# Memory attention and a bilinear feed-forward on one core: one block of ones for two buffers, and a new order of all units behind the first eighth

## The chip, the cores and the metric

The kernel runs on one core of a Trainium2 chip. The metric is the device time of one execution in microseconds (us), the median of several runs. TensorE is called PE, VectorE DVE, ScalarE ACT, GpSimd POOL and SyncE SP, as in the profile.

## The reference

Attention over 32 memory slots for 8 batches of 8 heads, 576 tokens of 64 numbers; its output is 4608 rows of 512, which go through a bilinear feed-forward with 1536 inner columns.

```python
a = np.exp(phi - max(phi)); a = a / sum(a)          # over the tokens
k_m = einsum('bhsm,bhsd->bhmd', a, k)               # 32 slots for each head
v_m = einsum('bhsm,bhsd->bhmd', a, v)
scores = q @ k_m^T / 8
attn = softmax(scores)                              # over the 32 slots
x = (attn @ v_m), heads side by side                # 4608 x 512
out = ((x @ w_a) * (x @ w_b)) @ w_out               # 512 -> 1536 -> 512
```

## The kernel before

The work runs batch by batch (b = 0 to 7). The attention's last product is never made alone: v_m is multiplied into w_a and w_b first ("folds", L516), so that one product of the softmax `A` with the folded weights `vab` gives the rows of `x @ w_a` and `x @ w_b`. The down projection with w_out takes blocks of 128 tokens in pairs, by seven products in the place of eight (L654); it needs sums of weights (L621) and of tokens (L638). For batches 5 to 7 most up projections are made by seven products too (L750), with sums of `vab` (L533) and of `A` (L541).

The ones: the sums over tokens of `a` come out of the same matmuls as k_m, since each buffer `kv_sb` holds three planes: k, v, and a constant (1/16). There are two such buffers, for even and odd b, and each has its constant plane; the first is written by VectorE (L236), the second by GpSimd (unit M, L792).

Nothing is ordered by a scheduler at run time: the string PLAN lists all units, and the loop at L785 records them in that order. Each engine then works through its own queue in that order, and waits by semaphore where it needs another's result. The names of units:

- `wa..`, `wb..`, `oN`, `pb`, `kb`, `vb`, `qb`: loads of w_a, w_b, w_out, phi, k, v, q, all issued by GpSimd's queue; at most eight of them are in flight, a ninth waits for the first to land.
- `2exp0`: exponentials of phi for b=2 (ACT); `2kv`: the sums with k, v and ones (PE, L323); `2km0`, `2km1`: their scaling (DVE); `2kvt`: transposes; `2qt0` to `2qt3`: transposes of q (DVE).
- `2sc`, `2e0`, `2den0`, `2nr0`: scores, exponentials, denominators and normalising; the last is a product on DVE for b below 2 and on POOL for b=2 and 3. From b=4 on `ed`, `sm`, `tn`, `ad` do it by transposes and row sums.
- `2v0a`, `2x0a0`: a fold into the first third of w_a, and one copy of it from PSUM.
- `a1.4.0`, `b1.4.0`: up projections with w_a and w_b (two matmuls each, L727) for batch 1, inner block 4, first half of the tokens; `a` is copied by ACT (L731), `b` multiplied by DVE into `ht` (L734).
- `P5.4.1`: one of the seven products; `H5.4` or `J5.4`: its closing product on POOL or DVE (L781).
- `V20`, `T30`: sums of w_out on DVE or POOL (quarter and half of it follow the letter); `5S01D`, `5S31P`: sums of `vab` on DVE or POOL; `5T0P`, `5T0D`: sums of `A` likewise.
- `g0.1`, `h0.1`: the sums of tokens for the pair of blocks 0, the second of four, on DVE or POOL.
- `d7`: the next seven matmuls of the down projection, 42 for each pair of blocks; after every sixth a result is taken by ACT or DVE.

```python
for x in PLAN.split():
    ...
    elif x[0] in "TV":
        sum_weights(int(x[1]), int(x[2]), nc.gpsimd if x[0] == "T" else nc.vector)
    elif x[0] in "hg":
        n, y = arg.split(".")
        sum_tokens(int(n), int(y), nc.gpsimd if x[0] == "h" else nc.vector)
    elif x[0] == "d":
        for _ in range(int(arg)):
            next(down)
```

Of the kernel before, what the change touches and what calls it, by code (L numbers as in the profile page):

```python
# [8 lines left out]
F32 = mybir.dt.float32  # L9
F16 = mybir.dt.float16  # L10
# [3 lines left out]
P = 128  # L14
# [9 lines left out]
1qh10 1qh00 o0 o3 1sh0 1eh00 0v1b 1v1b 1x0b1 1eh10 1x0a1 0x1b0 1den00 0x1b1 1x1b1 o4 1den10 o2 a0.6.1 b0.6.0 b0.6.1
b0.5.1 1nr10 1nr00 1x1b0 b0.4.0 a0.7.1 b0.7.1 a0.7.0 a0.5.0 b0.7.0 a1.5.0 b0.5.0 h0.3 b1.5.0 a1.3.0 1qh21 a0.4.1 o5
b1.3.0 1qh31 1qh01 a1.4.0 b0.4.1 a1.1.0 1qh11 a1.2.0 b1.4.0 a1.0.0 b1.1.0 1sh1 0v2a 1eh01 1eh11 0x2a1 b1.0.0 0x2a0
b1.2.0 1den01 a1.6.0 0v2b 0x2b0 0x2b1 b1.6.0 v2 a0.9.1 1v2b 1v2a 1x2b0 1x2b1 a0.11.1 1x2a1 1x2a0 b0.9.1 a0.10.1
a0.9.0 b0.11.1 b0.10.1 b0.9.0 V20 1den11 a1.10.0 b1.10.0 a0.11.0 b0.11.0 a0.8.0 a1.11.0 b0.8.0 b1.11.0 1nr11 d1
# [5 lines left out]
g2.3 2x2b1 3km0 2nr1 2x2b0 2x1a1 d7 3km1 d6 3qt2 2x1a0 2v0b 2v2a 2x0b1 3qt3 d3 3qt0 2x2a1 d3 a2.6.0 d1 b2.6.0 d1
3qt1 a2.4.0 2x2a0 b2.4.0 d1 h2.2 d1 a2.7.0 d2 a2.4.1 d1 2x0b0 b2.4.1 d4 a2.3.0 a2.1.1 3kvt 5exp1 v5 b2.7.0 p4 b2.3.0
a2.8.0 b2.1.1 k5 a2.1.0 d2 a2.2.0 d2 q4 d1 a2.5.0 h3.3 3sc 3e0 d2 b2.2.0 d1 3e1 d2 b2.8.0 5exp0 d1 b2.1.0 v4 d2
a2.10.0 d2 b2.10.0 a2.0.1 a2.11.0 b2.11.0 b2.5.0 3den0 a2.0.0 d1 b2.0.1 h3.0 d1 g3.1 a2.5.1 d1 a2.9.0 k4 b2.5.1 h3.2
b2.0.0 3nr0 a2.11.1 d1 a2.8.1 b2.9.0 d1 3den1 d2 a2.10.1 d2 b2.10.1 d1 3v0a 3nr1 3x0a1 5kv 3x0a0 3v0b 3x0b0 b2.8.1
# [35 lines left out]
a7.9.0 d1 P7.5.3 d2 P7.5.7 d1 J7.7 d1 g14.1 d1 P7.6.6 d1 P7.1.1 P7.6.5 P7.6.2 d1 7S20P d1 h14.2 P7.5.4 d3 P7.6.7
H7.5 d1 b7.11.0 P7.1.6 d1 h14.3 P7.1.5 P7.6.3 d1 P7.1.2 d2 P7.6.4 d1 P7.0.1 d1 P7.1.7 d1 H7.6 d1 b7.9.0 d1 P7.0.5 d1
P7.0.2 d1 P7.1.3 P7.0.6 d2 P7.1.4 P7.2.1 d2 P7.0.3 P7.3.1 d3 P7.0.7 P7.2.2 P7.2.6 P7.3.5 d3 P7.3.6 d2 J7.0 P7.2.5
P7.0.4 d1 H7.1 P7.2.7 d1 a7.10.1 P7.3.7 d5 P7.3.2 d2 P7.2.4 d3 P7.3.4 g15.0 d1 a7.8.1 d3 a7.9.1 g15.1 a7.11.1
b7.11.1 b7.9.1 d12 g15.2 g15.3 P7.2.3 b7.8.1 P7.3.3 d12 b7.10.1 d1 J7.3 H7.2 g16.0 d7 g16.1 g16.2 g16.3 g17.0 g17.1
d2 h17.2 d20 h17.3 d66
"""  # L80
# [3 lines left out]
def kernel(  # L84
# [196 lines left out]
    def units(b):  # L281
# [269 lines left out]
        def one(f, *a):  # L551
            return lambda: f(*a)
# [289 lines left out]
```

## Time and profile before

| what | value |
|---|---|
| median of 3 runs | 234.03 us (233.72 to 235.49) |
| profiled execution: span from first to last instruction | 232.1 us |
| PE busy | 214.1 us (92%) |
| DVE busy | 195.7 us (84%) |
| ACT busy | 169.4 us (73%) |
| POOL busy | 138.2 us (60%) |
| granted PE clock | 1.0 in all slices |

The profiled execution's own time is known by its span alone; the runs have 1.9 us more, which lies around it. A duration in a row is that of one instruction or of a merged run of them; PE's matmuls overlap, so that the distance between starts tells what one costs. Lines are those of the kernel before.

### The profile page before, as it was taken

The numbers are of one execution on the slowest core, as the hardware profiler recorded it, in microseconds if no ns is written. First come the engines' busy times: TensorE is split into PE (matmuls) and PEld (weight loads), VectorE is DVE, ScalarE is ACT, GpSimd is POOL, SyncE is SP. The second block draws the span as 40 slices with busy tenths as digits, with TensorE's granted clock in tenths as the row PEclk, the third lists the DMA queues.
The fourth block names the chain that finished last, engine by engine and source line by source line (L and its number), as shares of the span: only waits on it lengthen the run. The fifth ranks groups of instructions, "written<-read, shape, count | busy, mean of one in ns | idle before, by whom it ended". The sixth has DMA issues, their size and how long they took to land.

```text
span 232.1 us, 7493 instructions
## 1 busy us (share of the span) xinstructions
PE 214.1 (92%) x2906; PEld 163.6 (70%) x2906; DVE 195.7 (84%) x517; ACT 169.4 (73%) x450; POOL 138.2 (60%) x139
## 2 busy tenths in 40 slices
PE   1189879999999998999999999999999999999993
PEld 0143537588778777777777787887778877888882
DVE  3543899999987667898988999999999999999942
ACT  2206679987899997589978996977897769785330
POOL 7927233812549597893374099499475991881151
PEclk9999999999999999999999999999999999999999
DMA  6999999999998999999840902121303303032164
GB/s 229 238 199 256 205 205 205 205 259 258 208 284 138 264 207 243 253 241 254 210 93 4 190 1 65 28 64 32 93 3 90 78 16 92 18 77 55 42 158 111
DMA packets 26259, 34.09 MB, mean 147 GB/s; under 512 B 2000, under 2 KB 20304, under 8 KB 26224
## 3 DMA queue, kind: packets, MB, share of 16 engines
q0 software_dynamic: 19760, 23.14, 53.5%
q1 hardware_dynamic: 5952, 9.70, 16.2%
q10 hardware_dynamic: 512, 0.79, 1.0%
q8 instruction: 22, 0.36, 0.6%
q14 instruction: 13, 0.11, 0.1%
HBM read 42.47 MB, written 9.44 MB: 224 GB/s over the span
## 4 chain that ended last, share of the span: by engine, by line
PE 71%; DMA 17%; POOL 6%; ACT 3%; issue 2%; DVE 1%; POOLq 0%
PE py L654 18%; PE pb L727 11%; PE pa L727 11%; PE pv L654 9%; DMA wb_sb<-in_moe_w_b_dram 6%; DMA kv_sb<-in_k_dram 6%; PE py L750 5%; PE px L654 4%; PE pva L516 4%; DMA kv_sb<-in_v_dram 4%; PE pv L750 3%; POOL h_sums L638 2%; PE pkv L323 2%; PE px L750 1%; ACT vab L548 1%
## 5 line engine op out<-in xcount | busy, mean ns | idle before, releaser
L734 DVE TENSOR_TENSOR ht<-a_sb,pb 128x288 f16<-128x288 f16 (+2 forms) x144 | 60.5, 445 | 9.6 <-PE pb L727 5.3
L727 PEld LDWEIGHTS <-vab 128*128 128x128 f16 x576 | 55.3, 98 | 14.9 <-issue 2.4
L731 ACT CAST a_sb<-pa 128x288 f16<-128x288 f32 (+2 forms) x144 | 55.1, 417 | 13.6 <-PE pa L727 8.9
L727 PE MATMUL pb<-A,vab 128*128 128x288 f16 (+2 forms) x288 | 54.9, 286 | 0.1
L727 PE MATMUL pa<-A,vab 128*128 128x288 f16 (+2 forms) x288 | 54.3, 286 | 0.5 <-DVE A L478 0.4
L548 ACT CAST vab<-pva 128x512 f16<-128x512 f32 x82 | 45.4, 611 | 6.9 <-PE pva L516 6.8
L654 PEld LDWEIGHTS <-h_sums 128*128 128x128 f16 x432 | 41.4, 98 | 9.9 <-issue 2.4
L638 POOL TENSOR_TENSOR h_sums<-ht 128x768 f16<-128x768 f16 x19 | 31.2, 1645 | 21.4 <-DVE ht L734 21.3
L654 PE MATMUL py<-w_sums,h_sums 128*128 128x256 f16 x216 | 38.1, 273 | 0.0
L654 PEld LDWEIGHTS <-ht 128*128 128x128 f16 x324 | 31.2, 98 | 7.5 <-issue 2.2
L654 PE MATMUL pv<-wo_sb,h_sums 128*128 128x256 f16 x216 | 36.4, 273 | 0.0
L638 POOL TENSOR_TENSOR h_sums<-ht,h_sums 128x768 f16<-128x768 f16 x10 | 16.4, 1640 | 11.6 <-DVE h_sums L638 11.5
L755 ACT COPY z<-py 128x288 f32<-128x288 f32 x48 | 19.2, 415 | 2.3 <-PE py L750 1.8
L781 POOL TENSOR_TENSOR ht<-ah,bh 128x288 f16<-128x288 f16 x19 | 13.7, 737 | 10.1 <-DVE ah L759 7.1
L654 PE MATMUL px<-wo_sb,ht 128*128 128x256 f16 x108 | 18.9, 273 | 0.0
L654 PE MATMUL py<-wo_sb,ht 128*128 128x256 f16 x108 | 18.8, 273 | 0.0
L654 PE MATMUL py<-w_sums,ht 128*128 128x256 f16 x108 | 18.4, 273 | 0.0
L661 ACT ACTIVATE u<-py 128x256 f32<-128x256 f32 x36 | 14.4, 399 | 4.0 <-PE py L654 3.9
L425 ACT ACTIVATE E<-pscore 128x288 f16<-128x288 f32 x28 | 9.8, 431 | 9.5 <-PE pscore L412 9.4
L291 ACT ACTIVATE exp_sb<-phi_sb 128x576 f16<-128x576 f32 x16 | 10.9, 692 | 5.2 <-DMA phi_sb<-in_phi_dram 5.2
L300 DVE STREAM_TRANSPOSE qT<-q_sb 128x288 f32<-128x288 f32 x28 | 12.2, 456 | 2.6 <-DMA q_sb<-in_q_dram 2.6
L750 PE MATMUL py<-asum,vab 128*128 128x288 f16 x48 | 13.5, 286 | 0.0
(106 smaller groups left out, 383.0 us busy)
## 6 DMA issues: line engine op xcount, KB each, us to landing
out_dram<-o_sb SPq DMA_DIRECT2D x68, 128.0 KB, 2.4
phi_sb<-in_phi_dram POOLq DMA_DIRECT2D x8, 576.0 KB, 10.3
kv_sb<-in_v_dram POOLq DMA_DIRECT2D x8, 576.0 KB, 11.2
kv_sb<-in_k_dram POOLq DMA_DIRECT2D x7, 576.0 KB, 13.5
q_sb<-in_q_dram POOLq DMA_DIRECT2D x6, 576.0 KB, 11.9
wo_sb<-in_moe_w_out_dram POOLq DMA_DIRECT2D x6, 256.0 KB, 14.0
wa_sb<-in_moe_w_a_dram POOLq DMA_DIRECT2D x2, 512.0 KB, 14.2
wb_sb<-in_moe_w_b_dram POOLq DMA_DIRECT2D x2, 512.0 KB, 16.6
```

The costliest lines, as they stand in the source:

```text
L291: nc.scalar.activation(out=t["exp"][:, 2 * z:2 * z + 2, :, :], in_=phis[b][:, 2 * z:2 * z + 2, :].rearrange("p c (i m) -> p c i m", m=M), ...
L300: nc.vector.transpose(out=t["qT"][:, hp, :].bitcast(F32), in_=qs[b][:, hp, :].bitcast(F32))
L548: engine_copy(out=vabs[b][z][:, g, lo:hi], in_=pva[:, 0:hi - lo])
L638: engine.tensor_tensor(out=out, in0=in0, in1=in1, op=op)
L654: nc.tensor.matmul(po, lhs[:, i], rhs[:, i], start=first and i == 0, stop=i == KH - 1, skip_group_check=not first)
L661: nc.scalar.mul(out=x, in_=po, mul=scale)
L727: nc.tensor.matmul(ps, vabs[b][x][:, g, P * i:P * (i + 1)], attn[b][:, g, ts], start=(g == 0), stop=(g == 1))
L731: nc.scalar.copy(out=a_sbs[b, i, hf][:, :n], in_=ps)
L734: nc.vector.tensor_tensor(out=ht[:, i, t0:t0 + n], in0=a_sbs.pop((b, i, hf))[:, :n], in1=ps, op=ALU.mult)
L750: nc.tensor.matmul(x[bank][0], lhs, rhs, start=first, stop=True, skip_group_check=True)
L755: nc.scalar.copy(out=x[name], in_=po)
L781: engine.tensor_tensor(out=ht[:, i, t0 + HALF:t0 + S], in0=x["ah"], in1=x["bh"], op=ALU.mult)
```

## The change

One buffer `kv_all` of five planes takes the place of two of three: k and v of even batches, one plane of ones, k and v of odd batches. Both kinds of batches read three planes in a row, which share the one in the middle; for odd batches the ones come first. GpSimd's memset (M) is gone. The sums over tokens give up an unused variant (`slot_sums`), and units that sum k and v apart (`part_sums` and its followers) are added, which the list doesn't use. Three fixed buffers `vsum0` to `vsum2` become one pool of three that is handed round.

The list is the same through unit b0.9.0 but for M, and new behind it: the same units in another order, except that some sums change engine. On GpSimd instead of VectorE: V01 and V31 (as T01, T31), 5T0, 5T1, 5T3, 7T1, 7T3, and closing products 7.7, 7.0, 7.3; on VectorE instead of GpSimd: 5T2, 7T2, and closing products 5.4, 5.0. Of the sums of tokens and of `vab` as many are on each engine as before, though not the same ones: 38 and 34, 12 and 12.

```diff
 PLAN, the stretch behind b0.9.0 to 2kv
-V20 1den11 a1.10.0 b1.10.0 a0.11.0 b0.11.0 a0.8.0 a1.11.0 b0.8.0 b1.11.0 1nr11 d1
-1nr01 a0.10.0 d1 V00 a1.8.0 b0.10.0 a1.7.0 d1 b1.8.0 p2 V21 a1.11.1 b1.7.0 b1.11.1 d1 a1.3.1 a1.0.1 a1.2.1 g0.0 d1
-b1.3.1 a1.6.1 d1 b1.2.1 b1.0.1 V01 a0.8.1 V10 a1.4.1 a1.9.0 d1 k2 2exp0 2exp1 g0.1 d1 V11 b1.6.1 V31 a1.5.1 p3 g0.2
-b0.8.1 q2 d1 b1.4.1 d3 a1.1.1 b1.9.0 d6 2kv
+1nr01 a1.9.0 V20 V00 p2 1den11 a1.10.0 b1.10.0 a0.11.0 b0.11.0 k2 p3 q2 a0.8.0 a1.11.0 b0.8.0 k3
+b1.11.0 1nr11 d1 v3 d1 V21 q3 T01 d4 a1.7.0 b1.7.0 a1.8.0 b1.9.0 a1.4.1 a0.8.1 b1.8.0 b0.8.1 a0.10.0 b0.10.0 a1.3.1
+b1.3.1 a1.7.1 b1.7.1 a1.9.1 a1.8.1 g0.0 b1.4.1 2exp1 V10 a1.10.1 a1.6.1 b1.10.1 g0.1 V11 T31 g0.2 2exp0 a1.5.1 b1.5.1
+d2 T30 b1.6.1 a1.11.1 d3 b1.8.1 d3 2kv
 ...
 GpSimd's units from 2kv on to k4, in order
-k3 v3 h1.0 T30 q3 p5 2nr0 2nr1 h2.2 v5 p4 k5 q4 h3.3 v4 h3.0 k4
+h1.0 h2.0 p5 q4 2nr1 2nr0 k5 h2.1 v5 p4 h2.2 v4 h3.1 k4
 ...
 the loads behind k4
-q5 k7 p6 v6 q6 k6 p7 q7 v7
+q6 q5 p6 p7 v6 k6 q7 v7 k7
 ...
 the end
-H7.2 g16.0 d7 g16.1 g16.2 g16.3 g17.0 g17.1 d2 h17.2 d20 h17.3 d66
+H7.2 d4 g16.0 d4 g16.1 d12 g16.2 g16.3 g17.3 g17.0 d39 h17.1 d7 g17.2 d24
 ...
-    kv_sbs = [consts.tile([P, 3, NHP, NI * D], F16, name=f"kv_sb{t}") for t in range(2)]
-    kvs = [kv_sbs[b % 2] for b in range(B)]
+    kv_all = consts.tile([P, 5, NHP, NI * D], F16, name="kv_all")
+    kvs = [kv_all[:, 3 * (b % 2):3 * (b % 2) + 2] for b in range(B)]
+    trios = [kv_all[:, 2 * (b % 2):2 * (b % 2) + 3] for b in range(B)]
 ...
-    nc.vector.memset(kv_sbs[0][:, 2], 1.0 / CS)
+    nc.vector.memset(kv_all[:, 2], 1.0 / CS)
 ...
-            n = (3 - given) * D
-            t["pkv"] = [banks.take([P, 2 * D + (1 if given else D)], F32, "pkv", hold=True) for _ in range(2)]
+            t["pkv"] = [banks.take([P, 3, D], F32, "pkv", hold=True) for _ in range(2)]
 ...
-                            kvs[b][64 * r:64 * r + 64, 0:3 - given, hp, D * i:D * (i + 1)],
+                            trios[b][64 * r:64 * r + 64, :, hp, D * i:D * (i + 1)],
 ...
+            one, ks, vs = ((2, 0, 1), (0, 1, 2))[b % 2]
 ...
-                vsums[b, n] = spare.tile([P, 3, 512], F16, name=f"vsum{n}")
+                vsums[b, n] = vpool.tile([P, 3, 512], F16, name="vsum")
 ...
-            nc.gpsimd.memset(kv_sbs[1][:, 2], 1.0 / CS)
```

More of the change, by code (lines that the diff above doesn't have):

```diff
@@ L24 @@
[L24 to L28, printed above, removed]
@@ L34 @@
[L34 to L38, printed above, removed]
@@ L74 @@
[L74 to L78, printed above, removed]
@@ L79 @@
-d2 h17.2 d20 h17.3 d66
+wb0:256 0qt0 wa0:256 0qt3 wb256:512 0qt1 wa256:512 p1 0exp0 0exp1 F1 0ks0 0kt0 0ks1 0vs1 0vt1 0vs0 0vt0 k1 F1 0hv0a
+0s0 v1 0qt2 O 0kt1 0e0 F1 0s1 0e1 0hx0a0 0hx0a1 F2 0den10 0den01 0den11 0den00 wa512:1024 0hv0b 0hx0b0 0hx0b1 0hv1b
+0nr01 0nr10 0hx1b1 0nr11 0nr00 0hv1a 0hx1a0 q1.0 wb512:1024 0hx1a1 F4 a0.0.1 1exp1 a0.0.0 b0.0.0 0hx1b0 a0.1.1 b0.0.1
+1exp0 a0.3.1 b0.1.1 a0.3.0 a0.2.0 b0.3.1 b0.2.0 a0.2.1 b0.2.1 1kv a0.1.0 1km1 wa1024:1536 1km0 b0.3.0 q1.1 1kvt 0v1a
+0x1a0 0x1a1 1v0a 1v1a 1v0b 1x1a0 1x0a0 1x0b0 a0.5.1 1x1a1 1qh20 wb1024:1536 b0.1.0 o1 a0.6.0 1qh30 a0.4.0 1qh10 1qh00
@@ new lines @@
+o0 o3 1sh0 1eh00 0v1b 1v1b 1x0b1 1eh10 1x0a1 0x1b0 1den00 0x1b1 1x1b1 o4 1den10 o2 a0.6.1 b0.6.0 b0.6.1 b0.5.1 1nr10
+1nr00 1x1b0 b0.4.0 a0.7.1 b0.7.1 a0.7.0 a0.5.0 b0.7.0 a1.5.0 b0.5.0 h0.3 b1.5.0 a1.3.0 1qh21 a0.4.1 o5 b1.3.0 1qh31
+1qh01 a1.4.0 b0.4.1 a1.1.0 1qh11 a1.2.0 b1.4.0 a1.0.0 b1.1.0 1sh1 0v2a 1eh01 1eh11 0x2a1 b1.0.0 0x2a0 b1.2.0 1den01
+a1.6.0 0v2b 0x2b0 0x2b1 b1.6.0 v2 a0.9.1 1v2b 1v2a 1x2b0 1x2b1 a0.11.1 1x2a1 1x2a0 b0.9.1 a0.10.1 a0.9.0 b0.11.1
+b0.10.1 b0.9.0 1nr01 a1.9.0 V20 V00 p2 1den11 a1.10.0 b1.10.0 a0.11.0 b0.11.0 k2 p3 q2 a0.8.0 a1.11.0 b0.8.0 k3
@@ new lines @@
+b1.11.0 1nr11 d1 v3 d1 V21 q3 T01 d4 a1.7.0 b1.7.0 a1.8.0 b1.9.0 a1.4.1 a0.8.1 b1.8.0 b0.8.1 a0.10.0 b0.10.0 a1.3.1
+b1.3.1 a1.7.1 b1.7.1 a1.9.1 a1.8.1 g0.0 b1.4.1 2exp1 V10 a1.10.1 a1.6.1 b1.10.1 g0.1 V11 T31 g0.2 2exp0 a1.5.1 b1.5.1
+d2 T30 b1.6.1 a1.11.1 d3 b1.8.1 d3 2kv 2km1 3exp1 2km0 h1.0 d3 a1.0.1 d2 a1.1.1 d2 b1.1.1 d7 2kvt d3 2qt1 d2 2qt3 2qt0
+3exp0 a1.2.1 2v1b 2x1b1 2v0a 2x0a0 d1 2x0a1 b1.0.1 2qt2 b1.11.1 2x1b0 d10 h2.0 d1 2sc 2e0 2v2a p5 g1.1 2e1 b1.9.1 q4
+g1.3 d8 2den0 d1 2den1 d2 g1.2 g2.3 d1 b1.2.1 d3 2nr1 d1 2nr0 3kv 3km1 2v0b 2x2a1 d7 3km0 d7 2x0b1 d3 k5 3qt2 2x2a0
@@ new lines @@
+d1 J5.4 d2 5x2b1 d1 b4.3.1 d3 P5.1.6 P5.1.5 a5.10.0 d3 P5.2.1 7exp1 d3 P5.1.7 P5.2.5 d2 P5.1.3 d3 a4.4.1 P5.2.2 b4.6.1
+P5.1.4 b4.4.1 P5.2.6 P5.2.3 P5.6.5 P5.6.1 d1 a4.5.1 d1 h9.1 h9.2 H5.1 P5.2.7 d2 a4.8.1 H5.2 d3 P5.7.1 d1 P5.7.2 P5.6.6
+d3 P5.2.4 P5.7.6 P5.6.3 P5.7.5 b4.5.1 h9.3 d2 P5.6.7 H5.6 P5.3.1 P5.7.3 a5.10.1 P5.7.7 H5.7 a5.8.0 b5.8.0 P5.3.5
+P5.3.6 P5.6.2 b4.8.1 d4 P5.0.1 P5.3.7 a5.9.0 P5.7.4 P5.0.2 P5.3.3 P5.0.6 d1 P5.6.4 P5.3.2 d1 P5.3.4 h10.3 a5.8.1
+P5.0.5 P5.0.7 d4 6ad d6 6v0a 6x0a0 6v0b 6x0b0 h10.0 P5.0.3 P5.0.4 d3 6x0b1 d2 H5.3 b5.10.1 6x0a1 d2 7qt1 d1 7kv 7km0
@@ new lines @@
+h12.1 P6.6.6 d2 a6.9.0 P6.6.2 d1 P6.0.2 P6.0.4 H6.0 7tn0 P6.6.5 a6.9.1 P6.2.1 d1 P6.4.1 d1 P6.6.7 d2 P6.6.3 d1 H6.6 d1
+h12.2 d1 P6.2.5 d1 P6.2.6 P6.2.2 d2 P6.5.1 d2 P6.2.3 d2 P6.6.4 P6.2.7 P6.4.2 b6.8.0 P6.4.6 d4 H6.2 h12.3 d1 7ad d4
+P6.2.4 d2 P6.4.5 P6.5.6 P6.5.2 b6.9.0 d2 P6.4.3 P6.5.5 d2 P6.4.7 H6.4 d3 P6.7.1 P6.5.7 P6.5.3 H6.5 a6.10.1 d1 7T0P
+7T1P P6.7.5 P6.4.4 P6.7.6 P6.5.4 d6 P6.7.7 7v1b 7x1b1 7v0a P6.7.2 P6.7.3 P6.7.4 d7 7x0a0 7x1b0 d4 7x0a1 a6.11.1 P7.4.1
+7S01D 7v0b 7x0b0 g13.0 7T2D 7v2a 7v2b g13.3 d3 7S00D 7S11D 7x0b1 d3 g13.1 d3 7S21D d1 7x2b0 d3 g13.2 7x2a1 7S31D
@@ L80 @@
+P7.0.4 P7.2.5 P7.2.7 P7.3.6 d1 P7.3.2 P7.3.5 d4 P7.3.7 P7.2.3 P7.2.4 d5 a7.10.1 P7.3.4 g15.0 g15.1 g15.2 g15.3 d2
+b7.10.1 a7.11.1 P7.3.3 b7.11.1 a7.9.1 d3 b7.9.1 H7.3 d21 b7.8.1 d6 H7.2 d4 g16.0 d4 g16.1 d12 g16.2 g16.3 g17.3 g17.0
+d39 h17.1 d7 g17.2 d24
 """
@@ L323, in kv_sums @@
                         nc.tensor.matmul(
-                            t["pkv"][g][0][32 * j:32 * j + 32, 0:n],
+                            t["pkv"][g][0][32 * j:32 * j + 32],
                             t["exp"][64 * r:64 * r + 64, hp, i, :],
-                            kvs[b][64 * r:64 * r + 64, 0:3 - given, hp, D * i:D * (i + 1)],
+                            trios[b][64 * r:64 * r + 64, :, hp, D * i:D * (i + 1)],
                             start=(i == 0),
@@ L330, in kv_sums @@
                         )
-            for g in range(2 * given):
-                for j in range(4):
-                    r, hp = head(g, j)
-                    nc.tensor.matmul(
-                        t["pkv"][g][0][32 * j:32 * j + 32, 2 * D:2 * D + 1],
-                        t["es"][64 * r:64 * r + 64, hp],
-                        one_cs[64 * r:64 * r + 64],
-                        start=True,
-                        stop=True,
-                        tile_position=(64 * r, 32 * j),
-                    )
         def take_kv(gs=range(2)):
@@ L347, in take_kv @@
                 t["rphi"] = small.tile([P, 2], F32, name="rphi")
+            one, ks, vs = ((2, 0, 1), (0, 1, 2))[b % 2]
             for g in gs:
                 pkv, bank = t["pkv"][g]
-                nc.vector.reciprocal(out=t["rphi"][:, g:g + 1], in_=pkv[:, 2 * D:2 * D + 1])
-                km = pkv[:, 0:D].rearrange("p (d e) -> p e d", e=2).unsqueeze(2).to_broadcast([P, 2, 2, 32])
+                nc.vector.reciprocal(out=t["rphi"][:, g:g + 1], in_=pkv[:, one, 0:1])
+                km = pkv[:, ks].rearrange("p (d e) -> p e d", e=2).unsqueeze(2).to_broadcast([P, 2, 2, 32])
@@ L352, in take_kv, with part_sums @@
                 half = slice(D * g, D * (g + 1))
                 for out, x in ((t["rep"][:, 0:2, half].rearrange("p e (z d) -> p e z d", z=2), km),
-                               (t["rep"][:, 2, half], pkv[:, D:2 * D])):
+                               (t["rep"][:, 2, half], pkv[:, vs])):
                     nc.vector.tensor_scalar(out=out, in0=x, scalar1=t["rphi"][:, g:g + 1], scalar2=None, op0=ALU.mult)
                 banks.free(bank)
+        def part_sums(x):
+            planes = ((slice(0, 3, 2), slice(1, 2)), (slice(0, 2), slice(2, 3)))[b % 2][x]
+            t["part", x] = [banks.take([P, 2 - x, D], F32, "pkv", hold=True) for _ in range(2)]
+            for i in range(NI):
+                for g in range(2):
+                    for j in range(4):
+                        r, hp = head(g, j)
+                        nc.tensor.matmul(
+                            t["part", x][g][0][32 * j:32 * j + 32],
+                            t["exp"][64 * r:64 * r + 64, hp, i, :],
+                            trios[b][64 * r:64 * r + 64, planes, hp, D * i:D * (i + 1)],
+                            start=(i == 0),
+                            stop=(i == NI - 1),
+                            tile_position=(64 * r, 32 * j),
+                        )
@@ new lines, in take_part @@
+        def take_part(x, g):
+            if "rep" not in t:
+                t["rep"] = spare.tile([P, 3, P], F16, name="rep")
+                t["rphi"] = small.tile([P, 2], F32, name="rphi")
+            pkv, bank = t["part", x][g]
+            half = slice(D * g, D * (g + 1))
+            if x == 0:
+                one, ks = ((1, 0), (0, 1))[b % 2]
+                nc.vector.reciprocal(out=t["rphi"][:, g:g + 1], in_=pkv[:, one, 0:1])
+                km = pkv[:, ks].rearrange("p (d e) -> p e d", e=2).unsqueeze(2).to_broadcast([P, 2, 2, 32])
+                out = t["rep"][:, 0:2, half].rearrange("p e (z d) -> p e z d", z=2)
+            else:
+                km, out = pkv[:, 0], t["rep"][:, 2, half]
+            nc.vector.tensor_scalar(out=out, in0=km, scalar1=t["rphi"][:, g:g + 1], scalar2=None, op0=ALU.mult)
+            banks.free(bank)
@@ L358, in kv_transpose, with part_transpose @@
+        def part_transpose(x):
+            if "kvT" not in t:
+                t["kvT"] = mid.tile([P, 3, P], F16, name="kvT")
+            xs = (slice(0, 2), slice(2, 3))[x]
+            pT = banks.tile([P, 2 - x, P], F16, name="pT")
+            for y in range(2 - x):
+                nc.tensor.transpose(out=pT[:, y, :], in_=t["rep"][:, 2 * x + y], identity=ident)
+            nc.vector.tensor_copy(out=t["kvT"][:, xs], in_=pT)
         def kv_transpose():
@@ L370, in sums @@
                 t["rphi"] = small.tile([P, 2], F32, name="rphi")
-                t["kvT"] = spare.tile([P, 3, 512], F16, name="vsum0").rearrange("p z n -> p (z n)")[:, :6 * P].rearrange("p (x n) -> p x n", n=P)
+                t["kvT"] = vpool.tile([P, 3, 512], F16, name="vsum").rearrange("p z n -> p (z n)")[:, :6 * P].rearrange("p (x n) -> p x n", n=P)
             part = (slice(0, 3, 2), slice(1, 2))[x]
@@ L379, in sums @@
                         t["exp"][64 * r:64 * r + 64, hp, i, :],
-                        kvs[b][64 * r:64 * r + 64, part, hp, D * i:D * (i + 1)],
+                        trios[b][64 * r:64 * r + 64, part, hp, D * i:D * (i + 1)],
                         start=(i == 0),
@@ L472, in normalise @@
             if ("R", 0) not in t:
-                both = spare.tile([P, 3, 512], F16, name="vsum1").rearrange("p z n -> p (z n)")
+                both = vpool.tile([P, 3, 512], F16, name="vsum").rearrange("p z n -> p (z n)")
                 for x in range(2):
@@ L555, in units @@
             u[f"exp{z}"] = one(exp_phi, z)
-            u[f"ps{z}"] = one(slot_sums, z)
+            u[f"{'kv'[z]}p"] = one(part_sums, z)
+            u[f"{'kv'[z]}x"] = one(part_transpose, z)
+            for g in range(2):
+                u[f"{'kv'[z]}g{g}"] = one(take_part, z, g)
             u[f"ks{z}"] = one(sums, z, 0)
```

81 lines of the change are left out of this document (31 added, 50 removed).

## The prediction

> **What bounds the kernel now.** I read the engine totals and the slices first, then what TensorE waits for, then its timeline, then GpSimd's and VectorE's sums.
>
> ```profile
> PE 214.1 (92%) x2906; PEld 163.6 (70%) x2906; DVE 195.7 (84%) x517; ACT 169.4 (73%) x450; POOL 138.2 (60%) x139
> PE   1189879999999998999999999999999999999993
> PEclk9999999999999999999999999999999999999999
> ```
>
> PE is nearly full from the eighth slice on, at full clock. A busy PE need not be at its peak, so I took the distance from one matmul's start to the next:
>
> ```profile
> 222.63 0.82 PE L654 MATMUL py<-w_sums,ht 128*128 128x256 f16 x6
> 223.28 0.82 PE L654 MATMUL py<-wo_sb,ht 128*128 128x256 f16 x6
> ```
>
> Six matmuls of 256 columns start 0.65 us before the next six, so 0.109 us each; in the same way L727 with 288 columns takes 0.1225. From 41 us to the last matmul at 227.8 the starts of plain matmuls (L654, L727, L750) follow each other at these rates, with 0.35 us lost in all. So from 41 us PE has no holes worth naming but one:
>
> ```profile
> PE pkv L323 <- DMA kv_sb<-in_k_dram: 0.6, 1, 0.6
> ```
>
> ```profile
> 91.32 0.38 PE L654 MATMUL py<-w_sums,h_sums 128*128 128x256 f16 x2
> 92.30 0.94 PE L323 MATMUL pkv<-kv_sb,exp_sb 64*32 64x192 f16 x72 [0.59 <-DMA kv_sb<-in_k_dram]
> ```
>
> The key sums of b=4 start 0.98 us after a group of two that needs 0.22: 0.76 us lost while k4 lands (92.2, issued 77.85). The rest of PE's lost time lies ahead of 41 us, where the list is the same before and after:
>
> ```profile
> 0.00:24.00 24.00, 12.42 (x248) 5.84 (x249) 10.75 (x30) 6.60 (x15) 16.50 (x26) 1.00 1.11 230
> 24.00:41.00 17.00, 15.20 (x271) 9.62 (x270) 15.75 (x45) 13.89 (x38) 5.72 (x7) 1.00 1.27 205
> 41.00:92.00 51.00, 50.70 (x778) 38.98 (x754) 43.42 (x115) 46.08 (x124) 30.51 (x30) 1.00 1.13 229
> 92.00:213.00 121.00, 120.70 (x1509) 96.24 (x1510) 114.31 (x303) 97.91 (x262) 80.33 (x73) 1.00 0.42 93
> ```
>
> The columns are PE, weight loads, VectorE, ScalarE, GpSimd, clock, DMA share, GB/s. From 41 on PE has 0.3 us idle in each stretch, and VectorE is close behind (114.3 of 121).
>
> **The change, part by part.**
>
> *The block of ones.* GpSimd's memset of the second block ("M") goes.
>
> ```profile
> 8.48 0.77 POOL L152 DMA_DIRECT2D phi_sb<-in_phi_dram  x1
> 9.22 2.06 POOL L792 MEMSET kv_sb<- 128x2304 f16 x1
> 11.18 0.77 POOL L155 DMA_DIRECT2D kv_sb<-in_k_dram  x1
> ```
>
> k1 is issued 2.06 us earlier and v1 about 1.1 (its queue slot is free only when a load of q lands, at 10.5). But the phi load issued just ahead (8.48) lands at 21.2 and k1 at 23.9, the 2.7 us of one load behind another in a full queue: the DMA engines had work all along. After v1 GpSimd waits 4.19 us for VectorE's "ones" anyhow, so the later loads don't move. Gain 0; bounds 0 and 2.06 (were it all on the path). I take 0, since both covers are seen.
>
> *Work.* The units are the same but for the engine of some sums. On GpSimd: two quarters of the output weights (T01, T31, 1.62 each), three more sums of A (0.73), one more H (0.73), less M: 3.24 + 2.19 + 0.73 - 2.06 = +4.1 us on 138. VectorE loses 2 x 0.55 + 3 x 0.30 + 0.30 = 2.3 us on 196. PE's 2906 matmuls stay. Neither sum sets the end, since PE does; it would count if cover were gone.
>
> *Tile switches on PE.* A run of small-tile matmuls costs a fixed part besides its work: runs of 8, 16 and 24 folds (L516) take 0.45, 0.65 and 0.87 us from the matmul before to the one behind, so 0.21 for each 8 and 0.235 for the switch. One of 24, with the run behind it:
>
> ```profile
> 109.96 0.41 PE L516 MATMUL pva<-wa_sb,kvT 64*32 64x512 f16 x8
> 110.19 0.62 PE L516 MATMUL pva<-wb_sb,kvT 64*32 64x512 f16 x16
> 110.74 0.50 PE L654 MATMUL pv<-wo_sb,h_sums 128*128 128x256 f16 x3
> ```
>
> From unit b0.9.0 on the old list has 21 runs of such units, the new one 23, with as many matmuls. Cost 2 x 0.235 = +0.47 us.
>
> *The wait for k4.* Counted in PE's work, 4kv stands at 84.8 us in the old list and 83.2 in the new; the old one ran 7.1 to 7.5 us behind that count, so the new one wants k4 at about 90.3. In the new list q3 goes out ahead of T01 (at about 48, when its slot is free, and not 59.8), p5 and q4 follow at about 60 to 62, and the queue, which ran dry at 70 before, goes on. k4 stands behind 2nr0 (ends 69.3 as before), k5, v5, h2.1, p4, h2.2, v4, h3.1: 5 x 0.77 with k4 itself and 3 x 1.64, so its issue ends at about 78, as before. Ahead of it in the queue are k5, v5, p4, v4 from 70 on: 3 x 2.9 + 1.6 + 2.9 = 13.2 us, landing at 83 to 85. The wait goes: -0.76 (bounds 0 and -0.76).
>
> *Sums of VectorE and GpSimd.* In the old trace none of the 75 VectorE operations with two inputs in SBUF (L478, L533, L541, L621, L638, L781) overlaps a GpSimd tensor operation, and none is lengthened:
>
> ```profile
> L638 POOL TENSOR_TENSOR h_sums<-ht x19: 1632/1642/1673, 38.8 to 223.7; 128x768 f16<-128x768 f16 x19
> L638 DVE TENSOR_TENSOR h_sums<-ht x17: 535/549/559, 51.5 to 220.7; 128x768 f16<-128x768 f16 x17
> ```
>
> ```profile
> 56.65 1.63 POOL L638 TENSOR_TENSOR h_sums<-ht 128x768 f16<-128x768 f16 x1 [9.14 <-DVE ht L734]
> ```
>
> Between 43 and 56.65 GpSimd only issues loads while VectorE makes twelve such sums. The new list puts T01, T31 and T30 into that stretch. T01 starts when V21 ends; seven products (b..., 0.365 each, one input in PSUM) stand between V21 and g0.0, 2.6 us against 1.62. T31 starts when V11 ends, and VectorE's next is g0.2. VectorE starts its next operation 0.08 us before the one ahead ends, GpSimd 0.17 us after (g17.1 to h17.2: 221.89 to 222.06), so VectorE goes first and T31 waits: 0 for PE. If GpSimd won, VectorE would lose up to 1.62 there. Bounds 0 and +1.6; I take 0.
>
> The Trainium skill (SBUF — State Buffer, "Who interferes with whom") says that a VectorE instruction with two SBUF inputs and a GpSimd instruction that reads SBUF share a port, and the second fully waits for the first. The trace fits (no overlap in 75), but shows no wait that proves it; by that rule each new meeting costs VectorE up to one GpSimd sum, and without it none costs anything. That is a rival below.
>
> *Chains with less room.* g16.0 is now listed 8 matmuls (0.87 us) ahead of its use instead of 17. Behind the last product that it needs, VectorE has one output sum (0.335) and itself (0.55): done 0.1 to 0.2 us ahead. In the last block h17.1 (1.64 on GpSimd) is ready about 1 us before PE needs it. h4.3, h4.0, h4.1, h4.2 stand in a row on GpSimd (6.6 us), behind p7, which waits for ScalarE's exponentials of b=4; by the count they end 0.9 us or more ahead of use. Cover that holds: 0; were it gone, one GpSimd sum, 1.64.
>
> *Sum.* 232.1 - 0.76 + 0.47 + 0 = 231.8 us of span. The profiled execution is known by its span alone, 232.1; the median of the runs is 234.03, 1.9 us more, which I put around the span after as before: 231.8 + 1.9 = 233.7 us.
>
> **The rivals.**
>
> *Sums meet after all (slower).* The new list has 61 VectorE sums (38 g, 5 V, 12 S, 2 T, 4 J), and GpSimd is busy about 60% of the time. If one in seven starts under a GpSimd sum and waits half of it, that is 9 x 0.82 = 7.4 us of VectorE. From 92 to 213 VectorE is busy 94%, so it can't give back much; PE fills its banks and stands. I take half, 3.7: 233.7 + 3.7 = 237.4 us. It decides once the waits exceed VectorE's room by 2.7 us. For it: small changes of timing move every meeting. Against: the old list kept them apart in all 75 cases.
>
> *GpSimd's queue is late once (same).* It carries 4.1 us more, with loads between its sums. One sum late by its length: 233.7 + 1.6 = 235.3.
>
> *M was on the path (faster).* Then 2.06 us more come off: 231.6. For it: PE is half idle up to 24 us. Against: the full load queue and the 4.19 us.
>
> *The wait moves.* k4 no longer waits, but another load does: +0.76, 234.5; within the forecast.
>
> **How the numbers follow.** The forecast with the moved wait has 0.60, GpSimd late 0.14, sums meeting 0.22, M 0.04. One per cent, about what a measurement of this kernel can tell from no change, is 231.7 to 236.4. So faster 0.04, same 0.74, slower 0.22. The forecast's own range is 233.2 to 234.6. The range asked for goes down by the 0.35 us of small losses and half a us of M, to 232.8, and up to nearly the meeting sums, 237.2.
>
> **What would show it.** Right: PE waits for no load at 4kv; small-tile runs cost the same; VectorE's sums stay at 0.55 us without idle time ahead of them; the first 41 us unchanged. Wrong: VectorE idle or slow next to GpSimd sums, PE idle in new places after 41 us totalling over 2 us, or a head shorter by a microsecond or more.

## The result and the profile after

The changed kernel takes 243.05 us (median of 4 runs, 242.41 to 243.73) against 234.2 (233.72 to 235.49) for the kernel before on the same chip: a ratio of 1.0358, with a 95% interval of 1.0303 to 1.0413 (the ratio is taken from all fast runs of both kernels; that of the two medians is 1.0378). The forecast was 233.7 in a range of 232.8 to 237.2; it was wrong. The profiled execution has a span of 240.0 us in the place of 232.1. Line numbers are those of the kernel whose profile is shown. After the change L666 makes the sums of tokens (L638 before), L558 the sums of `vab`, L527 the last step of the softmax for b from 4 on, L809 the closing products, L649 the sums of w_out, L762 the products into `ht`, L755, L682 and L778 are the matmuls of the up projections, of the down projection and of the seven products.

The page of the changed kernel: totals of the engines, and two rows of the 40 slices.

```profile
PE 217.6 (91%) x2906; PEld 163.5 (68%) x2906; DVE 202.7 (84%) x511; ACT 169.9 (71%) x450; POOL 145.0 (60%) x144
...
PE   1289889999998999999999999799988999999993
...
PEclk9999999999999999999999999999999999999998
```

TensorE has as many matmuls as before at the same clock (but for the last slice), but the slices (6 us each) that begin at 72, 150, 174 and 180 us now show 8, 7, 8 and 8; before, there was a single 8 behind the first 40 us, at the wait for k4. VectorE is 7.0 us busier, though it was given 2.3 us less to do: it doesn't do more, it takes longer. GpSimd is 6.8 us busier, where 4.1 were expected; 2.1 of that is lengthening too, as will be seen. The table by stage tells where (columns as before: TensorE, weight loads, VectorE, ScalarE, GpSimd, clock, DMA share, GB/s):

```profile
0.00:24.00 24.00, 12.67 (x247) 5.82 (x248) 10.63 (x30) 6.60 (x15) 14.69 (x25) 1.00 1.11 229
24.00:41.00 17.00, 15.30 (x241) 9.69 (x239) 15.55 (x45) 13.62 (x38) 5.46 (x7) 1.00 1.27 205
41.00:92.00 51.00, 50.03 (x806) 38.05 (x808) 41.87 (x106) 45.48 (x122) 36.59 (x35) 1.00 1.18 239
92.00:213.00 121.00, 116.67 (x1440) 90.55 (x1421) 115.12 (x286) 93.95 (x250) 79.49 (x70) 1.00 0.41 89
```

For TensorE the first 41 us are nearly as they were; GpSimd has 1.8 us less there, its memset. From 41 to 92 TensorE idles 1.0 us (0.3 before), and from 92 to 213 4.3 us (0.3 before). Counted by the starts of its matmuls against their rates, TensorE's idle time grows from 33.8 to 41.6 us, by as much as the span. The list of TensorE's waits names what is new:

```profile
PE pa L755 <- DVE ht L762: 1.7, 1, 1.7
PE pb L755 <- DVE ht L762: 1.4, 2, 1.0
...
PE py L778 <- DVE ht L805: 1.0, 1, 1.0
PE px L778 <- DVE ht L762: 0.9, 1, 0.9
```

Five waits for VectorE in four rows, 5.0 us together, and no wait for a load. TensorE waits there for a bank of PSUM that VectorE has not yet emptied. The sums of tokens show what VectorE was doing (engine, operation, count: shortest, median, longest in ns):

```profile
L666 DVE TENSOR_TENSOR h_sums<-ht x20: 515/551/2326, 53.3 to 228.9; 128x768 f16<-128x768 f16 x20
...
L666 DVE TENSOR_TENSOR h_sums<-ht,h_sums x8: 548/556/1398, 55.8 to 231.3; 128x768 f16<-128x768 f16 x8
```

The median is what it was, 0.55 us; the longest was 0.559 before and is 2.326 now. The largest pair of lengthened operations, in the timeline of the three engines:

```profile
148.59 1.83 DVE L527 TENSOR_TENSOR E<-E,sum 128x512 f16<-128x512 f16 x1
150.34 1.74 DVE L809 TENSOR_TENSOR ht<-ah,bh 128x288 f16<-128x288 f16 x1
152.00 0.44 DVE L762 TENSOR_TENSOR ht<-a_sb,pb 128x288 f16<-128x288 f16 x1
...
148.23 1.64 POOL L666 TENSOR_TENSOR h_sums<-h_sums,ht 128x768 f16<-128x768 f16 x1 [2.79 <-DVE h_sums L666]
149.95 1.97 POOL L666 TENSOR_TENSOR h_sums<-ht,h_sums 128x768 f16<-128x768 f16 x1
...
150.29 0.49 PE L682 MATMUL py<-w_sums,h_sums 128*128 128x256 f16 x3
152.49 0.40 PE L755 MATMUL pa<-A,vab 128*128 128x288 f16 x2 [1.72 <-DVE ht L762]
```

6tn1 (L527, 0.68 us in most other places) and J5.4 (L809, 0.30) each begin under one of two GpSimd sums (h9.1, h9.2) and end 0.55 and 0.17 us behind it, that is their own length less some 0.13. By these ends they did nothing until GpSimd was all but done. Behind them stands a product that must empty a bank, and TensorE stands still for 1.9 us.

There are eight such operations on VectorE, all with both inputs in SBUF and each under a GpSimd operation: g3.0 (+1.77 us, at 73.3), 5S21D (+0.96, 133.5), 6tn1 (+1.15) and J5.4 (+1.43), g11.2 (+0.84, 172.2) and J5.0 (+0.95, 173.5), 7tn1 (+0.54, 181.9) and 6S31D (+0.95, 183.0): 8.6 us together, against the medians of the same forms in the last of the mended lists below. TensorE has a hole behind each of the first two and behind each pair: 1.13, 0.56, 1.88 + 0.25, 1.10 + 0.25 and 1.16 us, 6.33 together. (Another of 0.32 at 197 is not the meetings': it stays when they are gone.) In seven places GpSimd is lengthened, by 2.1 us in all; VectorE had begun first. The products into `ht` (L762) take one input from PSUM and one from SBUF; 74 of the 144 lie under GpSimd sums for 0.2 us or more, and none is over 0.49 us.

### The profile page after: what moved, and what is told of

The parts are those of the page before. It is cut to its first block, busy times and chain, and to the rows that moved or that the text cites. A ratio compares the mean times of both kernels' runs of the same rounds, so it can differ in the third digit from the quotient of the medians.

```text
span 240.0 us, 7491 instructions
## 1 busy us (share of the span) xinstructions
PE 217.6 (91%) x2906; PEld 163.5 (68%) x2906; DVE 202.7 (84%) x511; ACT 169.9 (71%) x450; POOL 145.0 (60%) x144
## 4 chain that ended last, share of the span: by engine, by line
PE 81%; DVE 9%; DMA 4%; issue 2%; ACT 1%; POOL 1%; DVEq 0%; POOLq 0%
PE py L682 18%; PE pb L755 14%; PE pa L755 14%; PE pv L682 9%; PE pva L541 5%; PE px L682 5%; PE py L778 5%; DMA kv_all<-in_v_dram 4%; PE pv L778 2%; PE pkv L314 2%; DVE h_sums L666 2%; PE pw L231 1%; DVE ht L762 1%; PE pscore L437 1%; PE px L778 1%
## 5 line engine op out<-in xcount | busy, mean ns | idle before, releaser
L755 PEld LDWEIGHTS <-vab 128*128 128x128 f16 x576 | 55.4, 98 | 19.7 <-issue 6.7
L762 DVE TENSOR_TENSOR ht<-a_sb,pb 128x288 f16<-128x288 f16 (+2 forms) x144 | 60.5, 443 | 9.1 <-ACT a_sb L759 4.7
L755 PE MATMUL pb<-A,vab 128*128 128x288 f16 (+2 forms) x288 | 55.5, 286 | 1.7 <-DVE ht L762 1.4
L755 PE MATMUL pa<-A,vab 128*128 128x288 f16 (+2 forms) x288 | 55.3, 286 | 1.9 <-DVE ht L762 1.7
L682 PEld LDWEIGHTS <-h_sums 128*128 128x128 f16 x432 | 41.4, 98 | 10.5 <-issue 3.0
L682 PE MATMUL py<-w_sums,h_sums 128*128 128x256 f16 x216 | 36.5, 272 | 0.0
L682 PEld LDWEIGHTS <-ht 128*128 128x128 f16 x324 | 31.0, 98 | 7.8 <-issue 2.6
L682 PE MATMUL pv<-wo_sb,h_sums 128*128 128x256 f16 x216 | 35.9, 273 | 0.0
L666 POOL TENSOR_TENSOR h_sums<-ht 128x768 f16<-128x768 f16 x16 | 26.1, 1641 | 8.4 <-DVE ht L762 8.4
L809 POOL TENSOR_TENSOR ht<-ah,bh 128x288 f16<-128x288 f16 x20 | 14.7, 738 | 15.5 <-DVE ah L787 12.9
L666 POOL TENSOR_TENSOR h_sums<-ht,h_sums 128x768 f16<-128x768 f16 x10 | 16.8, 1680 | 7.0 <-DVE h_sums L666 5.6
L682 PE MATMUL py<-w_sums,ht 128*128 128x256 f16 x108 | 18.3, 273 | 0.0
L682 PE MATMUL py<-wo_sb,ht 128*128 128x256 f16 x108 | 17.4, 273 | 0.0
L666 POOL TENSOR_TENSOR h_sums<-h_sums,ht 128x768 f16<-128x768 f16 x8 | 13.1, 1644 | 6.7 <-DVE h_sums L666 6.6
L682 PE MATMUL px<-wo_sb,ht 128*128 128x256 f16 x108 | 17.2, 273 | 0.0
```

The lines of the kernel that those rows point to most:

```text
L666: engine.tensor_tensor(out=out, in0=in0, in1=in1, op=op)
L682: nc.tensor.matmul(po, lhs[:, i], rhs[:, i], start=first and i == 0, stop=i == KH - 1, skip_group_check=not first)
L755: nc.tensor.matmul(ps, vabs[b][x][:, g, P * i:P * (i + 1)], attn[b][:, g, ts], start=(g == 0), stop=(g == 1))
L762: nc.vector.tensor_tensor(out=ht[:, i, t0:t0 + n], in0=a_sbs.pop((b, i, hf))[:, :n], in1=ps, op=ALU.mult)
L809: engine.tensor_tensor(out=ht[:, i, t0 + HALF:t0 + S], in0=x["ah"], in1=x["bh"], op=ALU.mult)
```

## The experiments

Theory A: VectorE operations with two SBUF inputs wait out GpSimd operations that read SBUF, the new list makes such meetings, and TensorE starves behind them. Theory B: the new order by itself, with GpSimd's greater load, makes things late. Theory C: the shared block and buffers make new waits. Each run below was compared with runs of the kernel before on its own chip (medians 234.0 to 235.0 us), and its ratio goes by these; medians of different sections compare less well.

### Code and list apart

```diff
 old_list_new_code: the changed kernel, PLAN of before without M
 new_list_old_code: the kernel before, PLAN of after
-0vt0 k1
+0vt0 M k1
```

> The changed code (one block of ones, one pool for the sums of vab, no memset on GpSimd) with the old list of units. Theory A (VectorE operations with two inputs in SBUF meet GpSimd operations that read SBUF; the new list makes the meetings): about the time before, 233.5 to 234.8 us, and no VectorE sum over 0.6 us. Theory B (the new order by itself, GpSimd's load): the same. Theory C (the shared buffers make new waits): about 243 us.

Measured: 234.2 us, ratio 0.9971 (0.9945 to 0.9996); no VectorE operation lengthened. GpSimd's queue in the head:

```profile
9.30 0.74 POOL L156 DMA_DIRECT2D kv_all<-in_k_dram  x1 [0.21 <-issue]
10.70 0.74 POOL L159 DMA_DIRECT2D kv_all<-in_v_dram  x1 [0.66 <-DMA q_sb<-in_q_dram]
16.81 0.31 POOL L261 TENSOR_SCALAR_AFFINE_SELECT ones<-ones 128x128 f16<-128x128 f16 x1 [5.37 <-DVE ones L260]
```

Without the memset k1 goes out 1.9 us earlier and v1 1.2, and then GpSimd waits for VectorE's ones 5.37 us instead of 4.19. What is behind starts when it did.

> The code before (two buffers, GpSimd's memset kept where it was) with the new list. Theories A and B: 242 to 244 us, with the same eight or so lengthened VectorE operations (8.7 us in all in the changed kernel). Theory C: about 234 us.

Measured: 241.95 us, just under the 242 expected, ratio 1.029 (1.0244 to 1.0336); the same eight operations are lengthened, by 8.6 us, here the pair of 148 us:

```profile
148.26 1.83 DVE L499 TENSOR_TENSOR E<-E,sum 128x512 f16<-128x512 f16 x1
150.01 1.74 DVE L778 TENSOR_TENSOR ht<-ah,bh 128x288 f16<-128x288 f16 x1
```

C falls: the new code costs nothing, and the list by itself brings the loss (2.9% here, 3.6% with the new code; the intervals overlap). A and B are not told apart by this.

### GpSimd work added under VectorE's sums

In the kernel before GpSimd idles for 9.14 us from 47.5 on, while VectorE makes eleven operations with two SBUF inputs.

```diff
 reads_at_sums
-2km1 v3 d3
+2km1 v3 X4 d3
 writes_at_sums
+2km1 v3 Y9 d3
 ...
+            for _ in range(int(arg)):
+                if x[0] == "X":
+                    same = ident.unsqueeze(1).to_broadcast([P, 6, P])
+                    nc.gpsimd.tensor_tensor(out=extras["scratch"], in0=same, in1=same, op=ALU.add)
+                else:
+                    nc.gpsimd.memset(extras["scratch"], 0.0)
```

> The kernel before, with four GpSimd sums of 768 columns added that read SBUF and that nobody needs (1.64 us each), in GpSimd's idle stretch from about 47.5 us on, where VectorE makes some eight sums with two inputs. The order of all other work is kept. Theory A: several VectorE sums there take 1 to 2 us in the place of 0.55, and the time grows by 2 to 5 us, to 236 to 239. Theories B and C (no such meeting matters): 234 us, VectorE's sums stay at 0.55.

Measured: 236.5 us, ratio 1.0074 (1.0037 to 1.0112); the span is 234.4. The timeline of GpSimd and VectorE there:

```profile
47.43 6.64 POOL L803 TENSOR_TENSOR vsum<-ident 128x768 f16<-128x768 f16 x4
...
49.20 1.82 DVE L620 TENSOR_TENSOR wo_sb<-wo_sb 128x768 f16<-128x768 f16 x1
...
51.70 1.05 DVE L620 TENSOR_TENSOR w_sums<-wo_sb 128x768 f16<-128x768 f16 x1
...
53.40 1.09 DVE L637 TENSOR_TENSOR h_sums<-ht 128x768 f16<-128x768 f16 x1
```

Three sums waited, 2.3 us in all (1.27 + 0.50 + 0.54), and the span grew by 2.3 (the time by 0.7%, or 1.7 us). TensorE has new holes right behind them, of 0.76, 0.69 and 0.39 us. The added operations read a constant and write a buffer that these three sums don't touch, so no exchange of data makes them wait. GpSimd's four operations follow each other within 0.1 us, and yet VectorE gets in each time behind the one that runs (its sums end 0.41 us behind the ends at 50.60, 52.34 and 54.07): here the one that waits goes next.

> The kernel before, with nine GpSimd memsets of 768 columns in the same place, which write SBUF and read nothing, and which nobody needs. Theory A, by the Trainium skill (SBUF - State Buffer, 'Who interferes with whom', where a GpSimd instruction that reads SBUF is the one that shares the port): 234 us, VectorE's sums stay at 0.55 us. If any GpSimd work in SBUF holds VectorE up: VectorE's sums there are lengthened and the time grows by 1 to 4 us.

Measured: 234.2 us, ratio 0.9981 (0.9943 to 1.0018).

```profile
47.48 7.12 POOL L805 MEMSET vsum<- 128x768 f16 x9
...
49.07 0.55 DVE L620 TENSOR_TENSOR wo_sb<-wo_sb 128x768 f16<-128x768 f16 x1
...
51.50 0.55 DVE L637 TENSOR_TENSOR h_sums<-ht 128x768 f16<-128x768 f16 x1
```

GpSimd works as long there, but reads nothing, and no sum of VectorE is lengthened. (The profiled execution is 1.2 us longer than that of before for another reason: k4, issued when it was, landed at 93.37, and TensorE waited 1.98 us for it.) This is what the Trainium skill (SBUF — State Buffer, "Who interferes with whom") says: a VectorE instruction with two SBUF inputs contends with a GpSimd instruction that reads SBUF, not with one that only writes it. The trace of before could not show it; these two runs agree with it. Their operations differ in length too (1.48 us by itself against 0.74), which was not varied alone.

### The same GpSimd work away from the sums

```diff
 reads_away: one X1 behind each of o2, k4, h6.3, v7 (kernel before)
 reads_away_2: one X1 behind each of k4, h6.3, v7
```

> The control to reads_at_sums: the kernel before with the same four added GpSimd sums that read SBUF (1.64 us each, needed by nobody), one each behind o2, k4, h6.3 and v7, where GpSimd stands idle and VectorE makes no sum with two SBUF inputs. Theory A (only a meeting costs): 234 us, no VectorE sum lengthened. Theory B (more GpSimd work costs by itself): 235.5 to 237, as with reads_at_sums (2.3 us of span more).

Measured: 239.4 us, ratio 1.0226 (1.0182 to 1.0269), with no VectorE operation lengthened. Against both expectations, and by a fault of the experiment:

```profile
43.48 1.47 POOL L803 TENSOR_TENSOR vsum<-ident 128x768 f16<-128x768 f16 x1 [8.64 <-PE pva L515]
...
59.21 0.94 PE L322 MATMUL pkv<-kv_sb,exp_sb 64*32 64x192 f16 x72 [3.07 <-ACT u L660]
```

The first added sum shares its place in SBUF with a buffer of the head, waits 8.6 us for it, and the loads behind it in GpSimd's queue go out some 6 us late (phi of b=2 at 47.99 instead of 41.86); TensorE stands for 3.2 us at 2kv. It shows what a wait in GpSimd's queue does to the loads, not what the sums cost.

> The control again, with the added GpSimd sums behind k4, h6.3 and v7 alone. Behind o2 the added sum had waited 8.6 us for its place in SBUF and held the loads back, so that run told nothing of theory B. Theory A: 234 us, no VectorE sum lengthened, no new hole of PE after 41 us. Theory B (GpSimd's work costs by itself, 2.3 us for four sums in reads_at_sums): 235.7.

Measured: 234.1 us, ratio 0.9976 (0.9949 to 1.0002); nothing lengthened.

```profile
79.10 1.48 POOL L803 TENSOR_TENSOR vsum<-ident 128x768 f16<-128x768 f16 x1
...
111.02 1.46 POOL L803 TENSOR_TENSOR vsum<-ident 128x768 f16<-128x768 f16 x1
```

Under the first of these VectorE makes products with an input in PSUM at their usual length. So these three sums cost nothing where they meet no sum of VectorE: the half of theory B that lies in the load falls, as far as 4.4 us of added work can tell.

### The new list mended

No unit changes its engine here, and the code is that of the changed kernel.

```diff
 first_four_apart: order of units moved
+ p4 behind h2.2; g3.0 behind b2.8.0; 5S21D and g8.1 behind b4.7.0; h9.1, h9.2 behind H5.1
 all_eight_apart: also
+ 6S10D behind J5.0; 7tn1, g12.0 behind P6.1.2; 6S11P behind h11.3; 6S31D ahead of P6.3.3
 all_apart_2: as all_eight_apart, but
+ 7tn1 behind P6.3.7; g12.0 behind P6.3.3
```

> The changed kernel with its list mended at the first four of the eight meetings: p4 behind h2.2 and g3.0 behind b2.8.0; 5S21D and g8.1 behind b4.7.0; h9.1 and h9.2 behind H5.1. No unit changes its engine. Theory A: the four lengthened VectorE operations (1.80 + 0.96 + 1.16 + 1.42 us longer) go back to their lengths, PE's holes behind them (1.13 + 0.56 + 1.88 + 0.25 = 3.8 us) close: 243.0 - 3.8 = 239.2 us, 238.5 to 240. Theory B (the order as such, GpSimd's load): 242 to 244. The other four meetings stay.

Measured: 238.3 us, just under the range of 238.5 to 240, ratio 1.0184 (1.0156 to 1.0212), span 236.5: 4.1 us less than the changed kernel by the ratios, 3.5 by the spans, where 3.8 was expected. Of the first four lengthenings 0.11 us is left (5S21D still begins under 5S31P, but near its end), the holes behind them are gone, and the other four are still there (3.3 us of VectorE).

> The same, with the other four meetings mended too: 6S10D behind J5.0, so that 6S20, 6S30 and 6S01 start later; 7tn1 and g12.0 behind P6.1.2; 6S11P behind h11.3 and 6S31D ahead of P6.3.3. Theory A: 8.7 us of VectorE's lengthening are gone, PE's holes of 3.8 + 1.10 + 0.25 + 1.16 + 0.32 = 6.6 us close: 236.4 us, 234 to 237. Theory B: 242 to 244.

Measured: 238.2 us, ratio 1.0168 (1.0131 to 1.0205), span 235.3. Outside what A expected: the four are gone, but the new place of 7tn1 made another.

```profile
174.86 1.40 DVE L527 TENSOR_TENSOR E<-E,sum 128x512 f16<-128x512 f16 x1
...
174.56 1.15 POOL L558 TENSOR_TENSOR vsum<-vab 128x512 f16<-128x512 f16 x1
...
177.15 0.28 PE L778 MATMUL py<-asum,vab 128*128 128x288 f16 x1 [1.29 <-DVE bh L787]
```

One sum lengthened by 0.72 us, with another one (g12.0, 0.55) listed behind it ahead of a bank that TensorE needed: 1.46 us of TensorE.

> As all_eight_apart, but 7tn1 behind P6.3.7 and g12.0 behind P6.3.3, since in that run 7tn1 met 6S11 instead (0.74 us longer) and held PE up for 1.46 us. Theory A: no VectorE operation is over 0.2 us longer, that hole shrinks to 0.5 us or less: 1.0 to 1.5 us less than all_eight_apart's 238.2, so 236.7 to 237.2. What then stays over 234 is not the meetings'. Theory B: 238.

Measured: 236.1 us, ratio 1.0065 (1.0033 to 1.0098), span 234.0; a little better than expected. The groups with two SBUF inputs (shortest, median, longest in ns):

```profile
L666 DVE TENSOR_TENSOR h_sums<-ht x20: 516/552/558, 53.5 to 222.9; 128x768 f16<-128x768 f16 x20
```

```profile
L527 DVE TENSOR_TENSOR E<-E,sum x4: 650/682/684, 108.9 to 175.9; 128x512 f16<-128x512 f16 x4
```

```profile
L809 DVE TENSOR_TENSOR ht<-ah,bh x4: 301/302/304, 146.5 to 197.0; 128x288 f16<-128x288 f16 x4
```

```profile
L558 DVE TENSOR_TENSOR vsum<-vsum,vab x3: 419/419/527, 133.4 to 195.9; 128x512 f16<-128x512 f16 x3
```

The 0.527 is 5S21D's rest. The same units on the same engines, and 2.9 of the 3.6% are gone with the meetings (6.0 of 7.8 us by the spans). What the new list keeps, 0.3 to 1.0% over before, is not the meetings': TensorE idles 35.6 us against 33.8, with 0.5 of the difference ahead of 41 us (where executions of the old list differ as much), 0.67 in two short waits (158.3 and 191.0), the rest in holes of under 0.2 us. I did not follow these further.

### The one gain that was named

```diff
 old_list_early_k4: the changed code, old list
-b2.0.1 h3.0 d1 g3.1 a2.5.1 d1 a2.9.0 k4
+b2.0.1 k4 h3.0 d1 g3.1 a2.5.1 d1 a2.9.0
```

> The changed code with the old list, in which only the load k4 is moved ahead of the sum h3.0 (1.64 us on GpSimd). It tests the one gain that the prediction named: PE's wait of 0.76 us for k of batch 4 in the kernel before. If the loads' own rate allows it, k4 lands up to 1.6 us earlier, PE waits 0 to 0.4 us: 233.2 to 233.7 us against 234.2. If the loads ahead of k4 set its landing: no change, 234.2. If h3.0 now comes late: up to 0.8 us slower.

Measured: 234.3 us, ratio 1.0012 (0.9988 to 1.0037). k4 goes out 1.6 us earlier than in old_list_new_code, which differs in this alone (76.75 instead of 78.33), and lands no earlier (92.35 against 92.12), 3.6 us behind v4 as there: the loads ahead of it set its landing. TensorE's wait there is 0.43 us. It was 0.25 in old_list_new_code, 0.76 before and 1.98 in writes_at_sums, so it changes by over a microsecond between kernels that issue k4 in the same place. No kernel here beats the kernel before by 1%, which is about what the measurement tells.

## Why the prediction was wrong

*The step that failed* is "Sums of VectorE and GpSimd", in its words "Bounds 0 and +1.6; I take 0". Its bounds came from one stretch, 43 to 57 us. There it was right, to the order of who goes first:

```profile
55.80 0.55 DVE L666 TENSOR_TENSOR h_sums<-ht,h_sums 128x768 f16<-128x768 f16 x1
...
55.97 3.49 POOL L649 TENSOR_TENSOR w_sums<-wo_sb,w_sums 128x768 f16<-128x768 f16 x2 [3.78 <-DVE w_sums L649]
```

g0.2 keeps its 0.55 us and T31, the first of the two, takes 1.89 instead of 1.63. But the list was new from there to the end, and the 170 us behind were not looked at for meetings. They came at 73, 133, 148 to 152, 172 to 175 and 182 to 184 us: 8.6 us of VectorE in the place of 0, and holes of 6.33 us in TensorE.

The observation that 75 operations never overlapped was read as evidence that meetings are rare, and set against the rival. (The list of 75 leaves out the four at L502, the last step of the softmax, which have both inputs in SBUF as well; they overlapped no GpSimd operation either. Two of the eight meetings, 6tn1 and 7tn1, are of this kind.) It was the reverse. In the kernel before GpSimd's long idle stretches are where VectorE's sums stand: 47.5 to 56.7 us with eleven of them, 61.4 to 66.8 with six, 126.4 to 133.9 with ten, 191.2 to 196.3 with eleven. With GpSimd busy 60% of the time, 75 misses hardly come by chance; the order kept them apart, and a new order, unless it does so too, loses that.

*The rival "Sums meet after all"* had the mechanism, and its price of VectorE's time nearly right: one in seven sums, 9 x 0.82 = 7.4 us, against one in eight (8 of 65, its 61 and the four of the softmax), 8 x 1.08 = 8.6. The term that was mis-sized is "I take half". TensorE lost 6.33 us in the holes behind the meetings, about three quarters: VectorE was already 94% busy from 92 to 213 us and gave only 2.3 back. The rival's own 7.4 in full would have given 241.1. Its chance, 0.22, stood on the observation that was misread.

*The block of ones:* taken as 0, bounds 0 and 2.06. Right: the changed code with the old list is at 0.9971 (0.9945 to 0.9996), 0.1 to 1.3 us less. Both covers were seen.

*Work:* GpSimd +4.1 and VectorE -2.3 us, "neither sets the end": reads_away_2 bears out that GpSimd's load costs nothing by itself.

*The wait for k4:* -0.76. Right as to the wait, which is gone in the changed kernel; but with the order of before it was 0.25 to 1.98 us in these runs, so much of it comes and goes by itself. The landing was forecast too early: k4 landed at 88.8, not at 83 to 85. The sum counts the loads' own rate from 70 on, but the first of them (k5) took 8.4 us from issue to landing.

```profile
91.41 0.27 PE L682 MATMUL pv<-wo_sb,h_sums 128*128 128x256 f16 x1
91.61 0.94 PE L314 MATMUL pkv<-kv_all,exp_sb 64*32 64x192 f16 x72
```

4kv starts 0.2 us behind the start of the matmul ahead, and waits for nothing.

*Tile switches* (+0.47): the traces bear it out. Behind 41 us TensorE has 24 runs of small-tile matmuls in old_list_new_code and 26 in the changed kernel, with 976 matmuls in each, and equal runs cost the same (16 folds 0.65 us, 24 folds 0.87). *Chains with less room* (0): no matmul waits for a sum of tokens in the changed kernel, one weight load does for 0.2 us. The mended list leaves 1.5 us by the ratio, into which +0.47 - 0.76 would fit only with over a microsecond of small holes that the sum did not have. The 1.9 us around the span is not fixed either: it is 1.9 to 3.2 in the four runs of the changed kernel.

*The rival "GpSimd's queue is late once":* not seen; TensorE waits for no GpSimd sum.

## What to carry to other kernels

Where two engines never overlap on a kind of operation, though both are busy most of the time, ask what keeps them apart: it may be the order, and a change of order then has to be checked for it over the whole list, not at the place where the diff is largest. A lengthened operation on an engine that is 94% busy reached the end by about three quarters here, since what stood behind it in its queue had to empty a bank for TensorE; half is no safe guess. An order written by hand is mended meeting by meeting, and each unit moved must be looked at in its new place.

## What the runs showed of the hardware

A VectorE operation with two SBUF inputs that begins under a GpSimd operation reading SBUF did nothing here until that had all but ended (5S21D ends 0.29 us behind 5S31P, with 0.42 of its own); its record in the trace is lengthened, it doesn't show as idle time. It works the other way too: GpSimd operations that began while VectorE held on were lengthened by 0.15 to 0.43 us. GpSimd memsets (0.74 us each, 0.79 from start to start) didn't do it, nor did an operation of VectorE with one input in PSUM suffer (at most 0.49 us).

One meeting stays unexplained. At 133.06 us the record of a VectorE sum (g8.0) begins 0.01 us ahead of GpSimd's, and VectorE goes first (0.55 us). At 73.3 us VectorE came first by its record, by 0.25 us, and lost:

```profile
73.31 2.33 DVE L666 TENSOR_TENSOR h_sums<-ht 128x768 f16<-128x768 f16 x1
...
72.76 0.78 POOL L151 DMA_DIRECT2D phi_sb<-in_phi_dram  x1
73.56 1.65 POOL L666 TENSOR_TENSOR h_sums<-ht,h_sums 128x768 f16<-128x768 f16 x1
```

g3.0 could have read from 73.4 on, when the product ahead of it ended, and GpSimd was then still issuing a load; yet it ran behind the sum that began at 73.56. Whether the load's issue held it, or GpSimd takes hold ahead of its record, was not tried. Elsewhere a load's issue alone lengthened no VectorE sum; in all_apart_2 g3.0 itself lies under two of them, at 0.55 us.
